# Folding the channels a second time ahead of a token transform, with the whole issue order from one table

## The chip, the core and the metric

The kernel runs on one core of a Trainium2 chip. A core has a matrix engine (TensorE, PE in the profile, with its weight loads as PEld), a vector engine (VectorE, DVE), a scalar engine (ScalarE, ACT), a general engine (GpSimd, POOL) and a queue engine that starts DMAs (SyncE, SP). Each works through its own list of instructions in order; semaphores tie them together. The metric is the device time of one launch in microseconds. The three runs of the kernel before have a median of 995.22 us (994.12 to 995.35).

## What is computed

Inputs are q, k, v of shape (8 batches, 8 heads, 576 tokens, 64), a gain g of 64 values and two weight matrices w1 (512 x 2048) and w2 (2048 x 512). The reference does, per batch:

```python
kv  = einsum('bhsd,bhse->bhde', k, v)
out = einsum('bhsd,bhde->bhse', q, kv)
x   = out / sqrt(mean(out*out, -1) + 1e-6) * g      # heads side by side: 576 x 512
X   = fft(fft(x, axis=tokens), axis=channels)
u   = x + real(X)
un  = (u - mean(u)) / sqrt(var(u) + 1e-6)
y   = u + maximum(un @ w1, 0) @ w2
```

The two transforms are done as matrix products with cosine and sine tables. Products that need more than one rounded 32-bit float (`fp32r` in the rows) are split into a high and a low part and done in three passes: high x high, high x low, low x high.

## The kernel before, in words

Eight batches go through an attention-and-transform stage of which PE does only a part, and 36 row tiles of 128 tokens go through the feed-forward stage (FFN), which is nearly all PE. Tokens are handled in nine blocks of 512. A block's "early" FFN work (three of the sixteen slices of the hidden layer) is issued between the steps of later batches; the other slices follow when all batches are done (from about 325 us on).

The steps of a batch, with the names that the rows use: `plan_kv` (L1197, `ps_k`) makes k-transposed times v; `plan_q` (L1273, L1279, `ps_q`) turns q; `plan_out` (L1304, `ps_o`; for the first batch `plan_first_out`, L1374) makes the attention output in three tiles t = 0, 1, 2 of 96 or 97 token pairs, a token s and its mirror 576 - s side by side in one row of the tile `x`; `plan_y` and L1490 normalise it. `plan_fold` then uses the symmetry of cosine and sine: L1501 (`ab`) adds channel d and channel 512 - d of the mirrored token, which leaves 256 channels; L1508 (`xe`, or `part` and `ps_xe`) makes the sum and the difference of the two tokens; L1514 and L1517 split them into high and low parts. A table called MODES says for each batch and tile whether L1508 and L1517 run on DVE (seven tiles) or on POOL (the other 17). L1495 on ACT keeps channel 0 apart for the mean (`x0`). `plan_seq` (L1532, for the first batch L1544) is the token transform: 290 columns, `ps_f<-cs`. Its result is split again into `pt`. `plan_chn` (L1586, `ps_f<-cd`) is the channel transform: for the cosine and for the sine part six matmuls with 128 rows, 96 or 97 weight columns and 258 moving columns. L1601 copies the cosine part, L1609 mixes cosine and sine parts with a sign into two results, L1619 and L1622 on POOL or L1628 and L1629 on DVE add them to `x`, and `plan_turn` (L1684, `ps_t`) turns the sum so that it becomes the input `unTh`, `unTl` (L1693, L1696) of the FFN, whose matmuls are L1012 (`ps_h`) and L1029 (`acc`), and in the late stage L2251.

`plan_spare` issues fill matmuls (L1084, `ps_s`), which compute nothing that is used. PE takes one when the planner has no better work ready.

The order is made when the program is built: every step is an `Op` with an engine, a cost and a rank; `Plan.go` plays the steps through in model time and takes for each free engine the ready step of lowest rank; MOVES shifts ranks, and SHIFTS moves single steps of the finished list or drops them.

## Time and profile before

| | |
|---|---|
| median of three runs | 995.22 us |
| profiled execution, span from first to last instruction | 993.5 us |
| PE busy in the span | 982.3 us, 99% |
| DVE, ACT, POOL busy | 690.1, 363.4, 397.6 us |
| fill matmuls (L1084) | 54 |
| channel transform matmuls (L1586) | 288, of 258 columns |

The span of the profiled execution is 1.7 us below the median of the runs, which also hold what lies before the first and after the last instruction. A matmul's busy time is its time from start to the modelled end, and matmuls overlap in the pipeline, so that the distance between starts, not the duration of one, tells how much of PE one matmul takes.

### The profile page before, as it was taken

What the parts mean: (1) busy time and instruction counts of PE and PEld (TensorE: products, weight loads), DVE (VectorE), ACT (ScalarE), POOL (GpSimd) and SP (SyncE); (2) the same over time, 40 slices, a digit from 0 to 9 for tenths busy, and PEclk for the clock granted to TensorE, in tenths of its full rate; (3) what the DMA queues carried; (4) which work ended last, traced back from release to release, by engine and by line L of the source; (5) the groups of instructions that cost most, each with busy time, mean ns of one, the idle gap of its engine ahead of it and who ended that gap; (6) DMA issues with size and microseconds to landing.
All of it is one profiled execution on the core that took longest, in us unless ns stands there. A gap on an engine that the chain in (4) does not pass through costs nothing.

```text
span 993.5 us, 17707 instructions
## 1 busy us (share of the span) xinstructions
PE 982.3 (99%) x6838; PEld 858.5 (86%) x6838; DVE 690.1 (69%) x1365; ACT 363.4 (37%) x731; POOL 397.6 (40%) x391
## 2 busy tenths in 40 slices
PE   8999999999999999999999999999999999999998
PEld 6888989988988888888888898989898888989897
DVE  4889886966667668767843786767676766767543
ACT  2466555655544333333332331323231313122221
POOL 1345443553554101434230372727272727263540
PEclk9899999999999999999999999999999999999999
DMA  9989797764453645565644515151525253424031
GB/s 231 236 222 271 210 275 230 200 161 165 144 195 117 267 168 192 181 252 211 225 170 159 201 44 212 44 212 53 202 81 187 100 171 115 153 107 149 1 127 43
DMA packets 111240, 166.06 MB, mean 167 GB/s; under 512 B 43710, under 2 KB 71666, under 8 KB 104756
## 3 DMA queue, kind: packets, MB, share of 16 engines
q1 hardware_dynamic: 103908, 149.06, 46.9%
q10 hardware_dynamic: 5328, 9.57, 2.6%
q0 software_dynamic: 1920, 6.29, 1.6%
q8 instruction: 54, 0.88, 0.4%
q14 instruction: 30, 0.25, 0.1%
HBM read 108.25 MB, written 56.64 MB: 166 GB/s over the span
## 4 chain that ended last, share of the span: by engine, by line
PE 94%; DMA 3%; SPq 1%; DVE 1%; issue 0%; ACT 0%; DVEq 0%; ACTq 0%
PE acc L1029 40%; PE ps_h L1012 20%; PE ps_h L2251 18%; PE ps_f L1586 4%; PE ps_f L1532 3%; PE ps_o L1304 3%; PE ps_k L1197 2%; PE ps_t L1684 2%; DMA vm<-in_v_dram 1%; PE ps_q L1279 1%; DMA draw<-in_dft_s_dram 1%; DMA qt<-in_q_dram 1%; PE ps_s L1084 1%; PE ps_o L1374 0%; SPq L1174 0%
## 5 line engine op out<-in xcount | busy, mean ns | idle before, releaser
L1029 PE MATMUL acc<-w,hh 128*128 128x512 f32 x1150 | 359.3, 394 | 0.0
L1029 PEld LDWEIGHTS acc<-w,hh 128*128 128x128 f32 x1150 | 205.7, 189 | 34.2
L1029 PE MATMUL acc<-w,hl 128*128 128x512 f32 x575 | 224.0, 390 | 0.0
L1021 ACT ACTIVATE hh<-ps_h 128x512 fp32r<-128x512 f32 x144 | 86.2, 598 | 345.8 <-DVE ps_h L2259 170.9
L1012 PE MATMUL ps_h<-unTh,w 128*128 128x512 f32 x576 | 179.3, 392 | 0.0
L1024 DVE SCALAR_TENSOR_TENSOR hl<-ps_h,hh 128x512 fp32r<-128x512 f32 x144 | 98.0, 684 | 92.1 <-ACT hh L1021 91.8
L1029 PEld LDWEIGHTS acc<-w,hl 128*128 128x128 f32 x575 | 108.0, 188 | 23.6
L1012 PEld LDWEIGHTS ps_h<-unTh,w 128*128 128x128 f32 x576 | 106.6, 188 | 21.3
L1012 PE MATMUL ps_h<-unTl,w 128*128 128x512 f32 x288 | 112.3, 390 | 0.0
L2211 POOL TENSOR_TENSOR up<-up 128x512 f32<-128x512 f32 x36 | 46.6, 1295 | 154.4 <-DMA up<-next_scr 119.2
L2259 DVE TENSOR_TENSOR ps_h<-part,ps_h 128x256 f32<-128x256 f32 x144 | 61.1, 425 | 40.9 <-ACT part L2264 23.3
L2259 DVE TENSOR_TENSOR part<-part,ps_h 128x256 f32<-128x256 f32 x108 | 45.4, 420 | 44.4 <-PE ps_h L2251 41.5
L1012 PEld LDWEIGHTS ps_h<-unTl,w 128*128 128x128 f32 x288 | 54.1, 188 | 11.5
L2224 POOL TENSOR_TENSOR uu<-uu,up 128x512 f32<-128x512 f32 x36 | 46.9, 1312 | 36.9 <-ACT up L2216 36.9
L1353 POOL TENSOR_TENSOR x<-x,gb 96x512 f32<-96x512 f32 (+1 forms) x26 | 33.8, 1311 | 45.0 <-ACT x L1320 45.0
L2264 ACT COPY part<-ps_h 128x256 f32<-128x256 f32 x36 | 13.4, 373 | 81.4 <-PE ps_h L2251 81.4
L1696 DVE TENSOR_TENSOR unTl<-ps_t,unTh 128x384 fp32r<-128x384 f32 (+13 forms) x80 | 34.0, 477 | 9.0 <-ACT unTh L1693 8.9
L2358 DVE SCALAR_TENSOR_TENSOR uu<-acc,bz,uu 128x512 f32<-128x512 f32 x35 | 25.0, 750 | 20.2 <-PE acc L1029 20.2
L1508 POOL TENSOR_TENSOR xe<-ab 96x256 f32<-96x256 f32 (+1 forms) x32 | 25.0, 797 | 34.0 <-DVE ab L1501 32.7
L1340 DVE TENSOR_REDUCE ss<-ps_o 96x8 f32<-96x512 f32 (+1 forms) x42 | 27.9, 682 | 14.1 <-ACT ps_o L1336 13.9
L1586 PE MATMUL ps_f<-cd,pt 128*96 128x258 f32 (+1 forms) x288 | 37.0, 283 | 0.0
L1586 PEld LDWEIGHTS ps_f<-cd,pt 128*96 128x96 f32 (+1 forms) x288 | 35.0, 162 | 1.3 <-DVE ss L1340 0.2
(226 smaller groups left out, 1875.9 us busy)
## 6 DMA issues: line engine op xcount, KB each, us to landing
raw<-in_moe_w_ch_dram SPq DMA_DIRECT2D x32, 512.0 KB, 3.9
unTh<-unT_scr SPq DMA_DIRECT2D x16, 1024.0 KB, 4.9
unTl<-unT_scr SPq DMA_DIRECT2D x16, 1024.0 KB, 7.3
qt<-in_q_dram SPq DMA_DIRECT2D x16, 576.0 KB, 6.7
unT_scr<-unTh SPq DMA_DIRECT2D x9, 1024.0 KB, 3.8
unT_scr<-unTl SPq DMA_DIRECT2D x9, 1024.0 KB, 7.3
part_scr<-part ACTq DMA_DIRECT2D x36, 256.0 KB, 4.0
next_scr<-part SPq DMA_DIRECT2D x36, 256.0 KB, 2.8
```

The source lines that it names most:

```text
L1012: nc.tensor.matmul(ps, w[c][:, kc * P : (kc + 1) * P], unT[a][:, kc, :], start=(kc == 0 and n == 0), stop=(kc == KC - 1 and n == 2),)
L1021: nc.scalar.activation(hh, ps, AF.Relu)
L1024: nc.vector.scalar_tensor_tensor(hl, ps, 0.0, hh.bitcast(F32), ALU.max, ALU.subtract)
L1029: nc.tensor.matmul(acc, hpair[a][:, i * P : (i + 1) * P], w[c], start=(first and n == 0), stop=(last and n == 2),)
L1304: nc.tensor.matmul(pss[s].t[:n, at : at + D], fqs[side].t[half, m, :n], kvt.t[half, m], start=True, stop=True,)
L1353: nc.gpsimd.tensor_tensor(v_, v_, gb[:n].unsqueeze(1).to_broadcast([n, H, D]), ALU.mult)
L1586: nc.tensor.matmul(ps.t[:n, :ND], pt.t[a][:, part, ch, offs[t] : offs[t] + n], cd[:, part, c, ch, :], start=(idx == 0), stop=(idx == 5),)
L1696: nc.vector.tensor_tensor(unTs[j].t[1][:, :, to], view()[:, :, lo:hi], unTs[j].t[0][:, :, to].bitcast(F32), ALU.subtract,)
L2211: lambda p=part: nc.gpsimd.tensor_tensor(p.t[:, 0], p.t[:, 0], p.t[:, 1], ALU.add),
L2224: lambda k=k, ut=ut, p=part: nc.gpsimd.tensor_tensor(ut.t[:, k], ut.t[:, k], p.t[:, 0], ALU.add),
L2251: nc.tensor.matmul(x(to), w.t[:, c, i, kk * P : (kk + 1) * P], rhs(a, kk), start=(kk == 0 and n == 0), stop=(kk == 1 and n == 2),)
L2259: return op("DVE", 415, URGENT, lambda: nc.vector.tensor_tensor(out(), a(), b(), ALU.add), d, bufs)
```

## The change

The channels are folded once more on the way into the token transform. After the first fold a tile has 256 channels; the change adds (and subtracts) channel m and channel 256 - m, which gives 128 channels for the even outputs and 128 for the odd ones. The token transform is as it was (two groups of 128 channels for each part). The channel transform has, for each part, three matmuls of 130 columns for the even outputs and three of 130 for the odd ones, in place of six of 258; each group of three now uses only one group of channels. Even and odd outputs lie apart in the PSUM bank and are brought together where L1601 and L1609 of before read them. The cosine and sine tables on the chip keep one group of 260 columns, rearranged to even and odd, with a correction of their last row on DVE. The value for the mean is now a sum of four channels on DVE in place of two on ACT. On the seven DVE tiles the last fold result lies in PSUM as before, and on the others in the buffer `ab`.

The planner with its ranks, shifts and model time is gone. The order of all steps is one list of numbers, read from first to last; steps that are not in it are not issued.

```diff
-SHIFTS = [
-    ("plan_spare.go/PE/-/-", 20, 0),
...
-MOVES = {
...
+ORDER = """
+5 242 222 389 215 234 226 213 4 38 18 13 26 23 25 390 391 392 0 227 216 2 209 219 211 218 212 401 210 208 221
...
     def run(self):
-        first = [o for o in self.ops if o.first]
...
+        seen = set()
+        line = [self.ops[int(n)] for n in ORDER.split()]
+        for o in line:
+            seen.add(o.n)
+            if any(a.n not in seen for a in o.after):
+                raise RuntimeError(f"{o.key} stands ahead of what it needs")
+        self.emit(line)
...
-    ND = DH + 2
+    ND = DH + 4
+    NH = ND // 2
...
-    cd = cst.tile([P, 2, 2, 2, ND], F32R, name="cd")
+    cd = cst.tile([P, 2, 2, 1, ND], F32R, name="cd")
...
+            def fit():
+                if part == 0:
+                    odd, far = raw.t[:, 1 : DH + 2 : 2], raw.t[:, DH + 3 : 2 * DH + 4 : 2]
+                    nc.vector.scalar_tensor_tensor(odd, far, last_row[:, 1:2], odd, ALU.mult, ALU.add)
+                nc.vector.tensor_scalar(raw.t[:, :ND], raw.t[:, :ND], last_row[:, 0:1], None, ALU.mult)
+
+            ld = [op("DVE", 600, r, fit, ld, [raw])]
...
         if quick:
-            ab, xe = e2_buf("ab"), bank_buf("ps_xe")
+            ab, xe = e2_buf("ab"), e2_buf("xe")
...
         def zero():
-            nc.scalar.activation(
-                x0[:n, t, b : b + 1], xv(0)[:, 0:1], AF.Identity, bias=xv(1)[:, 0:1]
-            )
+            nc.vector.tensor_reduce(x0[:n, t, b : b + 1], x.t[:n, :: DH], AX.X, ALU.add)
...
+        to = bank_buf("ps_xe") if quick else ab
+
+        def again(s):
+            def go():
+                o, a = two_of(to), two_of(xe)
+                m = P - s
+                eng.tensor_tensor(
+                    o[:, :, s * P : s * P + m], a[:, :, :m], a[:, :, DH - 2 : DH - 2 - m : -1],
+                    ALU.subtract if s else ALU.add,
+                )
+                if s:
+                    eng.tensor_copy(o[:, :, DH - 1 : DH], a[:, :, DH - 1 : DH])
+            return go
...
             def mm(part=part, ps=ps):
-                idx = 0
-                for ch in range(2):
-                    for a, c in passes:
+                for odd in range(2):
+                    ks = slice(odd * NH, (odd + 1) * NH)
+                    for i, (a, c) in enumerate(passes):
                         nc.tensor.matmul(
-                            ps.t[:n, :ND],
-                            pt.t[a][:, part, ch, offs[t] : offs[t] + n],
-                            cd[:, part, c, ch, :],
-                            start=(idx == 0),
-                            stop=(idx == 5),
+                            ps.t[:n, ks],
+                            pt.t[a][:, part, odd ^ part, offs[t] : offs[t] + n],
+                            cd[:, part, c, 0, ks],
+                            start=(i == 0),
+                            stop=(i == 2),
                         )
...
+        def bank_of(part):
+            return pss[part].t[:n, :ND].rearrange("p (r m) -> p m r", r=2)[:, : (W + 1) // 2]
...
-                    pss[s].t[:n, :W] if quick else pmv()[:, s], pss[1].t[:n, :W], sgn_t[:n, s, 0:1], me.t[:n, :W], ALU.mult, ALU.add
+                    to, bank_of(1), sgn_t[:n, s, 0:1], pairs_of(me), ALU.mult, ALU.add
```

The issue order changes on every engine. On PE, in the first batch, ahead of the first parts of the attention output (`ps_o`), these rows stood before (`ps_s` is the fill, `ps_k` the product of k and v, `ps_q` the turned q):

```order
L1197 MATMUL ps_k<-vr,kr 64x64 x2
L1084 MATMUL ps_s<-still 128x512 x6
L1197 MATMUL ps_k<-vm,km 64x64 x8
L1197 MATMUL ps_k<-vr,kr 64x64 x2
L1084 MATMUL ps_s<-still 128x512 x4
L1197 MATMUL ps_k<-vh,kh 64x64 x8
L1197 MATMUL ps_k<-vr,kr 64x64 x2
L1084 MATMUL ps_s<-still 128x512 x4
L1374 MATMUL ps_o<-kvt,fq 96x64 x16
L1374 MATMUL ps_o<-kvg,fq 96x64 x16
```

and these stand there now (lines of the changed kernel):

```order
L723 MATMUL ps_k<-vr,kr 64x64 x2
L723 MATMUL ps_k<-vh,kh 64x64 x8
L723 MATMUL ps_k<-vr,kr 64x64 x2
L900 MATMUL ps_o<-kvt,fq 96x64 x24
L900 MATMUL ps_o<-kvt,pt_190 96x64 x8
L799 MATMUL ps_q<-ident,qt 64x97 x8
L591 MATMUL ps_s<-still 128x512 x4
L900 MATMUL ps_o<-kvg,fq 96x64 x16
```

The fill between the useful matmuls is gone but for these four; 14 more stand at the very start, so that 18 are left of 54. The rest of PE's work ahead of the first FFN matmul (`ps_h`) is the same set of matmuls in another sequence, except for the 36 of the channel transform.

Those 36 begin, on PE in the first batch, like this before (`cd` is the table, `pt` the split result of the token transform):

```order
L1197 MATMUL ps_k<-vr,kr 64x64 x2
L1304 MATMUL ps_o<-kvt,fq 96x64 x16
L1304 MATMUL ps_o<-kvt,fq 97x64 x16
L1586 MATMUL ps_f<-cd,pt_688 96x258 x2
L1586 MATMUL ps_f<-cd,pt_689 96x258
```

and like this now:

```order
L723 MATMUL ps_k<-vr,kr 64x64 x2
L1127 MATMUL ps_f<-cd,pt_694 97x130 x2
L1127 MATMUL ps_f<-cd,pt_695 97x130
L1127 MATMUL ps_f<-cd,pt_694 97x130 x2
L1127 MATMUL ps_f<-cd,pt_695 97x130
```

The same number of matmuls, 130 columns wide, in the same pattern of two weights with the high and one with the low part. Every later batch has the same change.

On DVE, at the end of the first batch, where the low parts of the turned block (`unTl`) are made, these rows stood before:

```order
L1696 TENSOR_TENSOR unTl<-ps_t,unTh 128x4x74
L1446 RECIPROCAL rs_y<-rs_s 97x48
L1696 TENSOR_TENSOR unTl<-ps_t,unTh 128x4x21
L1696 TENSOR_TENSOR unTl<-ps_t,unTh 128x4x75
L979 TENSOR_TENSOR wa<-wa,ps_w 128x512
L1455 TENSOR_TENSOR ps_y<-rs_y,rs_s 97x48
L1490 TENSOR_TENSOR x<-x,ps_y 97x512 x2
L1490 TENSOR_TENSOR x<-x,ps_y 96x512
```

and these stand there now:

```order
L1016 TENSOR_TENSOR x<-x,ps_y 96x512
L1016 TENSOR_TENSOR x<-x,ps_y 97x512
L866 TENSOR_REDUCE ss<-ps_o 96x2x4 x2
L1247 TENSOR_TENSOR unTl<-ps_t,unTh 128x4x74
L1016 TENSOR_TENSOR x<-x,ps_y 97x512
L1247 TENSOR_TENSOR unTl<-ps_t,unTh 128x4x96
L1247 TENSOR_TENSOR unTl<-ps_t,unTh 128x4x21 x2
L1247 TENSOR_TENSOR unTl<-ps_t,unTh 128x4x75
L1247 TENSOR_TENSOR unTl<-ps_t,unTh 128x4
L1247 TENSOR_TENSOR unTl<-ps_t,unTh 128x4x96 x2
L1247 TENSOR_TENSOR unTl<-ps_t,unTh 128x4x74
L1247 TENSOR_TENSOR unTl<-ps_t,unTh 128x4x22
```

Three scalings of the second batch's tiles (`x<-x,ps_y`) stood behind the last low part and stand ahead of it now; so do the centring of a weight slice (`wa<-wa,ps_w`) and the product `ps_y<-rs_y,rs_s`, which now stand eight and five rows ahead of the first row shown.

## Rows read from the trace of the kernel before

**Rows 1.** The page: busy us, share of the span and instructions of PE.
```profile
PE 982.3 (99%) x6838; PEld 858.5 (86%) x6838; DVE 690.1 (69%) x1365; ACT 363.4 (37%) x731; POOL 397.6 (40%) x391
```

**Rows 2.** The page, chain that ended last: shares of the span by engine.
```profile
PE 94%; DMA 3%; SPq 1%; DVE 1%; issue 0%; ACT 0%; DVEq 0%; ACTq 0%
```

**Rows 3.** Busy time by stretch: PE, PEld, DVE, ACT, POOL (instructions), granted clock, DMA.
```profile
34.50:41.50 7.00, 7.00 (x72) 6.04 (x70) 5.21 (x12) 3.45 (x9) 2.83 (x3) 0.52 1.17 206
41.50:78.80 37.30, 36.80 (x566) 33.00 (x562) 33.54 (x67) 21.31 (x50) 16.78 (x22) 1.00 0.86 225
78.80:150.00 71.20, 71.20 (x751) 63.60 (x750) 62.06 (x130) 42.04 (x98) 35.36 (x50) 1.00 0.89 255
150.00:225.00 75.00, 75.00 (x750) 67.38 (x749) 53.42 (x105) 42.49 (x100) 34.97 (x41) 1.00 0.66 192
225.00:316.00 91.00, 91.00 (x632) 79.33 (x631) 62.35 (x128) 46.54 (x105) 41.91 (x48) 1.00 0.43 154
```

**Rows 4.** PE in order of time: start, us, instruction, idle before it and releaser.
```profile
33.35 0.81 PE L1374 MATMUL ps_o<-kvg,fq 64*97 64x64 f32 x13 [1.17 <-ACT fq L1283]
37.51 2.07 PE L1084 MATMUL ps_s<-still 128*128 128x512 f32 x4
...
78.81 0.73 PE L1012 MATMUL ps_h<-unTh,w 128*128 128x512 f32 x2
...
79.61 1.09 PE L1084 MATMUL ps_s<-still 128*128 128x512 f32 x4
```

**Rows 5.** The fill line L1084: count, duration ns, first and last start.
```profile
L1084 PE MATMUL ps_s<-still x54: 389/400/793, 1.7 to 255.3; 128*128 128x512 f32 x54
```

**Rows 6.** PE in order of time, a channel transform of one batch and what follows.
```profile
268.95 4.46 PE L1586 MATMUL ps_f<-cd,pt 128*97 128x258 f32 x36
273.25 0.62 PE L1029 MATMUL acc<-w,hh 128*128 128x512 f32 x2
```

**Rows 7.** PE in order of time, matmuls of 512 columns, three to a group.
```profile
81.22 0.62 PE L1012 MATMUL ps_h<-unTh,w 128*128 128x512 f32 x2
81.67 0.39 PE L1012 MATMUL ps_h<-unTl,w 128*128 128x512 f32 x1
81.90 0.62 PE L1012 MATMUL ps_h<-unTh,w 128*128 128x512 f32 x2
```

**Rows 8.** Weight loads by shape: count, busy us, mean ns of one.
```profile
L1012 PEld LDWEIGHTS ps_h<-unTh,w 128*128 128x128 f32 x576 | 106.6, 188 | 21.3
...
L1586 PEld LDWEIGHTS ps_f<-cd,pt 128*96 128x96 f32 x192 | 23.6, 162 | 0.8 <-DVE ss L1340 0.2
...
L1964 PEld LDWEIGHTS ps_o<-cs,x0h 96*8 96x8 f32 x4 | 0.4, 89 | 0.2
```

**Rows 9.** PE in order of time: 96 weight columns, 64 moving columns, two halves.
```profile
52.30 1.57 PE L1304 MATMUL ps_o<-kvt,fq 64*96 64x64 f32 x32
53.81 0.88 PE L1273 MATMUL ps_q<-ident,qt 96*64 96x96 f32 x16
```

**Rows 10.** PE in order of time: plain float32, 128 columns, 4 products in 8 records.
```profile
76.22 1.16 PE L970 MATMUL ps_w<-wa,mean_t 128*128 128x128 f32 x8
77.31 0.90 PE L1304 MATMUL ps_o<-kvt,fq 64*96 64x64 f32 x16
```

**Rows 11.** DVE in order of time, the last low part of the first batch.
```profile
78.36 0.68 DVE L1696 TENSOR_TENSOR unTl<-ps_t,unTh 128x84 fp32r<-128x84 f32 x2
```

**Rows 12.** DVE by line and shape: count, busy us, mean ns of one, idle before.
```profile
L1490 DVE TENSOR_TENSOR x<-x,ps_y 96x512 f32<-96x512 f32 x28 | 18.3, 675 | 0.0
...
L1455 DVE TENSOR_TENSOR ps_y<-rs_y,rs_s 97x48 f32<-97x48 f32 x7 | 1.6, 226 | 4.3 <-POOL fq L1289 3.5 <-POOL rs_s L1452 0.8
...
L1696 DVE TENSOR_TENSOR unTl<-ps_t,unTh 128x4 fp32r<-128x4 f32 x8 | 1.2, 156 | 0.0
```

**Rows 13.** The line L1508 on POOL and DVE: count, duration ns minimum, median, maximum.
```profile
L1508 POOL TENSOR_TENSOR xe<-ab x32: 720/734/1358, 33.4 to 298.9; 96x256 f32<-96x256 f32 x20, 97x256 f32<-97x256 f32 x12
L1508 DVE TENSOR_TENSOR ps_xe<-ab x14: 415/430/1395, 93.8 to 210.6; 96x256 f32<-96x256 f32 x12, 97x256 f32<-97x256 f32 x2
```

More of the change, by code (lines that the diff above doesn't have):

```diff
@@ L566 @@
+ORDER = """
[183 rows of a table added]
+"""
 class Buf:
@@ L604, in __init__ @@
         self.ops = []
-        self.now = 0
         self.where = ("-", "-")
@@ L609, in op @@
         o = Op()
-        o.port = port or eng == "POOL"
-        o.wait = wait
         o.eng, o.cost, o.emit, o.lag = eng, cost, emit, lag
@@ L615, in op @@
         o.key = (f"{what}/{b}", f"{what}/{b}/{t}")
-        o.rank = rank + sum(MOVES.get(k, 0) for k in o.key)
         o.after = [a for a in after if a is not None]
@@ L1109, in plan_dft, with taken, laid @@
                 ))
+        want = size
+        if key == "d":
+            want = ND
+            def fit():
[4 more added lines that the diff above has]
+            ld = [op("DVE", 600, r, fit, ld, [raw])]
+        def taken():
+            v_ = raw.t[:n, :want]
+            return v_.rearrange("p (m r) -> p r m", r=2) if key == "d" else v_
+        def laid(a):
+            return a.rearrange("p (r m) -> p r m", r=2) if key == "d" else a
         aside = MODES.get(f"high/{key}{part}", 0)
@@ L1626, in add_q @@
         def add_q(s):
-            v_, w = xv()[:, s], pss[1 - s].t[:n]
-            nc.vector.tensor_tensor(v_[:, :W], v_[:, :W], pss[s].t[:n, :W], ALU.add)
+            v_, w = xv()[:, s], mixed[1 - s].t[:n]
+            nc.vector.tensor_tensor(v_[:, :W], v_[:, :W], mixed[s].t[:n, :W], ALU.add)
             nc.vector.tensor_tensor(v_[:, W:], v_[:, W:], w[:, DH - 1 : 0 : -1], ALU.add)
         if quick:
-            adds = [op("DVE", 720, r, lambda s=s: add_q(s), pms, [x] + pss) for s in range(2)]
+            adds = [op("DVE", 720, r, lambda s=s: add_q(s), pms, [x, me] + pss, port=True) for s in range(2)]
         else:
```

712 lines of the change are left out of this document (25 added, 687 removed), and 182 rows, old and new, of the table ORDER.

## The prediction

> **What bounds the kernel now.** I read the page first. PE is busy for 982.3 of 993.5 us, and its share of the chain that ended last is 94% [rows 1, 2]: matmul time taken out counts nearly in full wherever PE is dense. The windows tell where that is. From 78.8 to 316 us PE's busy time equals the length of each stretch, at granted clock 1.00, with DVE at 62 of 71, 53 of 75 and 62 of 91 us and POOL at half or less [rows 3]. Ahead of 78.8 us the busy PE misleads. [...] The first FFN matmul starts at 78.81 us; of the 54 fill matmuls 48 stand ahead of it and 6 behind, four at 79.61 us and the last at 255.3 [rows 4, 5]. So I split the span: time = T1, the start of the first FFN matmul, plus PE's work behind T1. The first part is set by the chain, the second by how many matmuls there are and how far apart they start.
>
> **Channel transform.** 36 matmuls of 258 columns take from 268.95 to 273.25 us: 4.30 us, 119.4 ns each [rows 6]. At 512 columns three start in 0.68 us, 226.7 ns each [rows 7]. So a column costs (226.7 - 119.4)/254 = 0.422 ns, and 130 columns would stream in 119.4 - 128 x 0.422 = 65.3 ns. That is one end, if nothing else limits. But each matmul loads its own 96 or 97 weight columns. A load of 96 took 162 ns, one of 8 took 89 [rows 8], so a column adds 0.83 ns and 96 of them about 80 ns, more than the stream. The nearest row with as little streaming is the attention output: 96 weight columns, two halves side by side, 32 records in 1.51 us, thus 94 ns a pair, with the change of form at its end [rows 9]. I take 84 ns, close to the load's 80 and below the 94. The other end is far: a plain float32 product of 128 columns stands as two records, and seven of eight records take 1.16 - 0.288 = 0.87 us, 125 ns each or 250 ns a product [rows 10] (0.288 us is the mean duration of one). No fp32r matmul narrower than 256 columns is in the trace, so rows do not exclude that the narrow ones fall to this.
>
> Of 288 matmuls, 36 belong to the first batch, ahead of T1, where 36 x 35.4 ns = 1.3 us go into waits. The other 252 lie where PE is dense: 252 x (84 - 119.4) = **-8.9 us**. The ends are -13.6 us at 65.3 ns and +32.9 us at 250 ns; 94 ns would give -6.4.
>
> The row shows loads hidden under the running matmul: 119.4 ns is what 258 columns need, though 80 ns of load go with each [rows 6, 8]. [...]
>
> **Fill.** The six behind T1 go: 6 x 0.227 = **-1.4 us** [rows 5, 7]. The 30 that go ahead of T1 free gaps, not the chain.
>
> **T1.** The first batch's end is on DVE: its last low part starts at 78.36 us and the first FFN matmul follows at 78.81 [rows 4, 11]. DVE is busy for 33.54 of the 37.3 us from 41.5 to 78.8 [rows 3], so work put ahead of that low part moves T1. There are now three scalings of 0.675 us, one product of 0.226 and the centring, in whose place I set 0.68, a like 512-column operation: 2.9 us, which stood behind [rows 11, 12]. Added are three small reductions for the mean, about 0.156 each, and the correction of the table's last row, about two operations of 0.68: 1.8 us. Removed is half of the table's low part, some 0.7 us, and the table's high part on ACT shrinks likewise. That is +4.1 us on an engine with 3.8 us of idle time there. Also, the second fold of the first batch goes to POOL: per tile 2 x 0.734 us and a small copy, about 1.6 us [rows 12, 13], in series before `xh` can be made, with the token transform on PE queued behind it and the two other tiles behind it on POOL. Against that, the whole stretch is ordered anew, 30 fill matmuls no longer stand ahead of ready work, and the channel transform is 1.3 us shorter. From above +5 us if nothing is hidden; from below -4, about the idle time that DVE has there. I take **+1.0 us**, since most of it has idle time to go into.
>
> **Hidden behind T1.** DVE gets 14 second folds at 0.43 to 1.395 us (6.0 to 19.5), 7 small copies and 21 reductions at 0.156 (4.4), and the 42 mixes that read with a stride cost at most what a mirrored read costs more per element in these rows, 0.430/256 against 0.675/512 us, 0.09 each (up to 3.8): 10 to 28 us in all [rows 12, 13]. From 78.8 to 316 us DVE is idle for 9.1, 21.6 and 28.7 us [rows 3]; PE's queue of ready FFN slices hides this, so nothing. POOL gets 28 folds of 0.734, 20.6 us, and their small copies, against 125 us of idle time: nothing, except by the chains they lengthen, which FFN work covers. The table's loads shrink; ACT loses 24 small steps.
>
> **Sum.** 993.5 - 8.9 - 1.4 + 1.0 = 984.2 us of span. The median lies 1.7 us above the profiled span: 985.9, so I say **986.0 us**. Within this likeliest case 84 may be 94 or 70 ns and T1 move by some us: 980 to 992.
>
> **Rivals.**
> A: the weight load hides entirely, matmuls start every 65 ns, and the new order brings T1 forward by 2 us. For it: loads are hidden today [rows 6, 8]. Against: 80 ns of load do not fit under 55 ns of streaming. 993.5 - 13.6 - 1.4 - 2 + 1.7 = 978. [...]
>
> B: DVE paces the batches behind T1. Eight of the 14 second folds come in the stretch from 78.8 to 150 us; if each takes the longest 1.395 us of its line, with a third of the other 8.2 us, DVE needs 62.06 + 11.2 + 2.5 = 75.8 of 71.2 us [rows 3, 13]. PE is late by 4.6: 990.5. Against: the median is 0.430, not 1.395.
>
> C, the slower side: a narrow fp32r matmul is run like plain float32, 250 ns for 130 columns. 993.5 + 32.9 - 1.4 + 1.0 + 1.7 = 1027.7. The point where the change stops paying is 121 ns per matmul, only 1.6 ns above today's. For it: both kinds of product on few columns that the trace has, [rows 9, 10], are slower per column than the wide ones and no row has a single-pass product this narrow. Against: nothing in the rows says that the width, not the plain float32, makes the two records.
>
> D: load and stream add up, 135 ns: 993.5 + 3.9 - 1.4 + 1.0 + 1.7 = 998.7, slower too. Against: 119.4 ns today.
>
> E: with fill gone between the first matmuls PE is quieter, and the granted clock stays near the 0.52 seen at 34.5 to 41.5 us for another such stretch [rows 3]. If PE sets the pace in it, 7 us more: 993, no change. Against: PE mostly waits for others there.
>
> That the new order does less than the old cannot be: the matmuls other than fill are the same ones, but for their width.
>
> **Chances.** Forecast 0.50 (986), A 0.20 (978), B 0.08 (990.5), C 0.12 (1028), D 0.04 (998.7), E 0.06 (993). About 0.2%, 2 us, is what a measurement of this kernel tells from no change. Faster: 0.49 of the forecast, A whole, 0.06 of B, 0.02 of E, 0.77. Within 0.2%: 0.01, 0.02 of B, 0.03 of E, 0.06. Slower: C, D and 0.01 of E, 0.17. The range goes from 975, three below A, to 999, which takes in D; C is left out.
>
> **What would show it.** The distance between starts of the 130-column matmuls decides: near 84 the forecast, 65 A, 135 D, 250 C. The first FFN matmul should start at 79 to 81 us; later by 3 or more, with DVE or POOL as releaser, and the T1 term was wrong; a longer stretch at half clock ahead of it is E. Behind it PE's busy time should still equal each stretch's length and DVE rise to 75 to 90% before 150 us; idle PE with a DVE releaser there is B. If the span shrinks with spacing and T1 as said, the sum is right; if it shrinks elsewhere, it is wrong.

## The result and the profile after

The changed kernel takes 1005.55 us, the median of 16 runs (997.53 to 1011.0). The kernel before, in the same sessions, takes 995.41 us (993.93 to 997.27, 16 runs). The ratio is 1.009, its 95% interval 1.0068 to 1.0112: about 10 us slower, where 986.0 had been forecast. The profiled execution took 1004.67 us and its span is 1002.9.

The first two lines of the page of the changed kernel that matter, busy time by engine and the chain that ended last, answer to [rows 1, 2]:

```profile
PE 973.8 (97%) x6802; PEld 849.2 (85%) x6802; DVE 704.0 (70%) x1415; ACT 353.1 (35%) x707; POOL 419.3 (42%) x442
...
PE 86%; DVE 5%; DMA 4%; POOL 2%; issue 1%; ACT 1%; SPq 0%; DVEq 0%; POOLq 0%; ACTq 0%
```

PE has less to do, 973.8 us for 982.3. But it is idle for 1002.9 - 973.8 = 29.1 us where it was idle for 11.2. That is 17.9 us more idle time against 8.5 us less work, and the difference is the 9.4 us by which the span grew. DVE, DMA and POOL, together 4% of the chain before, hold 11% of it.

Where the idle time lies is read from the windows of the changed kernel: the stretches of [rows 3], then four short ones picked for their clock. The columns are as there (PE, PEld, DVE, ACT, POOL, granted clock, DMA share, GB/s).

```profile
34.50:41.50 7.00, 6.09 (x118) 5.60 (x114) 6.79 (x19) 2.32 (x7) 5.26 (x10) 1.00 0.92 273
41.50:78.80 37.30, 31.37 (x495) 28.36 (x495) 36.71 (x73) 22.63 (x50) 20.76 (x31) 0.95 0.77 193
78.80:150.00 71.20, 67.96 (x733) 60.48 (x733) 60.01 (x125) 36.27 (x81) 37.61 (x56) 0.91 0.86 234
150.00:225.00 75.00, 74.84 (x750) 65.41 (x749) 60.44 (x134) 42.11 (x95) 33.69 (x46) 1.00 0.77 211
225.00:316.00 91.00, 91.00 (x669) 79.20 (x668) 63.16 (x138) 44.23 (x101) 60.22 (x78) 1.00 0.42 147
10.00:16.50 6.50, 6.02 (x58) 5.83 (x60) 1.02 (x2) 0.00 (x0) 0.00 (x0) 0.50 1.07 235
75.00:85.00 10.00, 9.63 (x89) 8.54 (x90) 9.38 (x20) 3.00 (x7) 0.72 (x1) 0.50 0.33 102
127.00:132.50 5.50, 5.44 (x68) 5.13 (x70) 5.43 (x11) 3.03 (x8) 1.74 (x3) 0.50 0.79 249
464.00:467.00 3.00, 3.00 (x9) 2.33 (x8) 1.86 (x3) 1.07 (x2) 0.37 (x1) 0.50 0.96 311
```

From 41.5 to 78.8 us DVE is busy for 36.71 of 37.3 us, where it had 3.8 us of slack: by these numbers it is now the engine with least room there. From 78.8 to 150 us PE no longer fills its stretch. In four places the granted clock is 0.50; the kernel before has one such place, at 0.52, the first row of [rows 3].

PE in order of time, in the changed kernel, from the transform of the first batch to the first FFN matmul (`ps_h`), with the idle time before a group and its releaser in brackets:

```profile
73.58 0.55 PE L1235 MATMUL ps_t<-ident,x 96*128 96x96 f32 x4 [2.13 <-DVE x L1180]
75.37 0.91 PE L1235 MATMUL ps_t<-ident,x 97*128 97x97 f32 x4 [1.25 <-DVE ss L866]
...
79.38 2.87 PE L830 MATMUL ps_o<-kvt,fq 64*97 64x64 f32 x32
...
82.79 1.20 PE L516 MATMUL ps_h<-unTh,w 128*128 128x512 f32 x2
...
86.06 1.57 PE L830 MATMUL ps_o<-kvt,fq 64*96 64x64 f32 x32
```

The first FFN matmul starts at 82.79 us, 4.0 us later than in [rows 4]. It stands behind two waits for DVE, and the clock, 0.96 from 72 to 75 us, was 0.50 from 75 on: the 32 records at 79.38 take 2.87 us, a like 32 at 86.06, at full clock, 1.57.

The waits of PE in the whole of the changed kernel, longest first (us in total, times, longest):

```profile
PE ps_w L474 <- DVE wa L1294: 3.0, 1, 3.0
PE ps_t L1235 <- DVE unTl L1247: 2.9, 1, 2.9
PE acc L533 <- ACT part L1897: 2.4, 1, 2.4
PE ps_t L1235 <- DVE x L1180: 2.1, 1, 2.1
PE ps_k L723 <- DMA km<-in_k_dram: 1.9, 2, 1.4
PE ps_s L591 <- DVE still L583: 1.8, 1, 1.8
PE ps_h L516 <- ACT part L1420: 1.6, 1, 1.6
```

Three of them lie behind the first FFN matmul, in the stretch that the forecast took for full: the second ends at 127.06 us, the last at 363.18, the third at 462.81.

```profile
127.06 1.52 PE L1235 MATMUL ps_t<-ident,x 96*128 96x96 f32 x8 [2.94 <-DVE unTl L1247]
...
462.81 0.73 PE L533 MATMUL acc<-w,hh 128*128 128x512 f32 x2 [2.38 <-ACT part L1897]
```

At these two lie the last two of the stretches at clock 0.50; the first stretch lies at the longest wait of all, 3.0 us for `wa`. In the kernel before, the longest wait behind that point was 1.1 us:

```profile
PE ps_h L2251 <- DVE bz L2113: 1.1, 1, 1.1
```

The narrow matmuls themselves do what was forecast. PE in order of time, one run of 18 of them at full clock, and what follows:

```profile
238.41 1.67 PE L1127 MATMUL ps_f<-cd,pt 128*96 128x130 f32 x18
239.91 0.68 PE L533 MATMUL acc<-w,hh 128*128 128x512 f32 x2
```

(239.91 - 238.41)/18 = 83 ns each, against 119.4 in [rows 6] and 84 in the forecast. Load and stream one after the other, 80 + 55 = 135 ns by the forecast's estimates (55 for 130 columns at 0.422 ns), are not what the trace shows.

The last thing that the totals of the page hide is one form on DVE. The adds that end the transform (L1179, L1180) take one mixed output from PSUM (`ps_f`) and the other from the buffer `me` in SBUF. Count, duration in ns (minimum/median/maximum), first and last start, first of L1179, then of L1180:

```profile
L1179 DVE TENSOR_TENSOR x<-x,ps_f x8: 407/412/417, 67.2 to 209.1; 96x257 f32<-96x257 f32 x6, 97x257 f32<-97x257 f32 x2
L1179 DVE TENSOR_TENSOR x<-x,me x8: 412/420/1511, 69.3 to 212.2; 96x257 f32<-96x257 f32 x6, 97x257 f32<-97x257 f32 x2
```

```profile
L1180 DVE TENSOR_TENSOR x<-x,me x8: 409/418/1391, 67.6 to 209.4; 96x255 f32<-96x255 f32 x6, 97x255 f32<-97x255 f32 x2
L1180 DVE TENSOR_TENSOR x<-x,ps_f x8: 404/406/413, 69.6 to 212.6; 96x255 f32<-96x255 f32 x6, 97x255 f32<-97x255 f32 x2
```

The same add takes 0.40 to 0.42 us with an input in PSUM, always, and up to 1.51 us with both in SBUF. Of those 16, eleven take 0.41 to 0.44 us and five take 0.74 to 1.51, 4.2 us more in all. DVE in order of time, and then POOL in the same microseconds, show when:

```profile
70.40 1.39 DVE L1180 TENSOR_TENSOR x<-x,me 96x255 f32<-96x255 f32 x1
71.72 1.48 DVE L1179 TENSOR_TENSOR x<-x,me 97x257 f32<-97x257 f32 x1
73.12 0.40 DVE L1180 TENSOR_TENSOR x<-x,ps_f 97x255 f32<-97x255 f32 x1
```

```profile
70.10 1.41 POOL L1319 TENSOR_TENSOR w<-wa,w 128x512 fp32r<-128x512 f32 x1 [1.62 <-ACT w L1314]
...
71.52 2.82 POOL L879 TENSOR_TENSOR x<-x,gb 96x512 f32<-96x512 f32 x2
```

POOL's first operation ends at 71.51 us and the first of its next two at 71.52 + 1.41 = 72.93. DVE's two adds end at 71.79 and 73.20, each 0.27 to 0.28 us behind. So it is with all five: each starts while a two-input operation of POOL runs and ends 0.27 to 0.28 us behind its end. They waited for POOL's operation, and PE's wait of 2.13 us for `x` ends with the add behind them, at 73.52. The trace shows this on DVE's side, by the five adds; that POOL waits for DVE in turn is not shown here. In the kernel before, both mixed outputs lay in PSUM.

### The profile page after: what moved, and what is told of

Read it like the earlier page. It is cut to its first block, busy times and chain, and to the rows that moved or that the text cites. A ratio compares the mean times of both kernels' runs of the same rounds, so it can differ in the third digit from the quotient of the medians.

```text
span 1002.9 us, 17683 instructions
## 1 busy us (share of the span) xinstructions
PE 973.8 (97%) x6802; PEld 849.2 (85%) x6802; DVE 704.0 (70%) x1415; ACT 353.1 (35%) x707; POOL 419.3 (42%) x442
## 4 chain that ended last, share of the span: by engine, by line
PE 86%; DVE 5%; DMA 4%; POOL 2%; issue 1%; ACT 1%; SPq 0%; DVEq 0%; POOLq 0%; ACTq 0%
PE acc L533 38%; PE ps_h L1802 18%; PE ps_h L516 17%; PE ps_f L1073 3%; PE ps_o L830 3%; PE ps_f L1127 2%; PE ps_k L723 2%; PE ps_t L1235 2%; DMA qt<-in_q_dram 1%; DMA km<-in_k_dram 1%; PE ps_q L805 1%; DMA uu<-u_scr,rowidx 1%; DMA part_scr<-part 1%; DVE x L1180 1%; PE ps_o L900 0%
## 5 line engine op out<-in xcount | busy, mean ns | idle before, releaser
L1247 DVE TENSOR_TENSOR unTl<-ps_t,unTh 128x384 fp32r<-128x384 f32 (+14 forms) x80 | 34.2, 468 | 10.7 <-ACT unTh L1244 10.7
L450 DVE TENSOR_SCALAR ps_a<-ps_a 128x512 f32<-128x512 f32 x32 | 22.1, 693 | 26.4 <-ACT ps_a L443 26.4
L1244 ACT ACTIVATE unTh<-ps_t 128x384 fp32r<-128x384 f32 (+16 forms) x80 | 34.4, 496 | 15.6 <-PE ps_t L1235 14.4
L1319 POOL TENSOR_TENSOR w<-wap,w 128x512 fp32r<-128x512 f32 x10 | 12.9, 1292 | 62.0 <-ACT w L1314 62.0
```

Source lines behind the costliest of these rows:

```text
L1244: nc.scalar.activation(unTs[j].t[0][:, :, to], view()[:, :, lo:hi], AF.Copy)
L1247: nc.vector.tensor_tensor(unTs[j].t[1][:, :, to], view()[:, :, lo:hi], unTs[j].t[0][:, :, to].bitcast(F32), ALU.subtract,)
```

## The experiments

Times are medians; the ratio is to the kernel before in the same session (995.3 to 996.1 us), with its 95% interval, and is not the quotient of the two medians. Profiles are one execution each.

**The new fold in the old order** (e1). The arithmetic of the change, with its steps issued in the order of the kernel before and its 54 fills:

```diff
-ORDER = """   (the changed kernel's sequence)
+ORDER = """   (the sequence of the kernel before; each second fold behind its first fold)
```

> The second fold alone, with the issue order (and the fill) of the kernel before; its new steps stand right behind the first fold's. Theory O (the new order is what costs: less fill, waits of PE, then half clock; the fold by itself pays): the first FFN matmul at 79 to 82 us, no new waits of 2 us behind it, 252 matmuls 34 ns closer, so 985 to 991 us, 0.990 to 0.996 of the kernel before. Rival F (the fold's added work on DVE and POOL makes PE late in any order): 1000 us or more, with waits of PE on DVE and POOL between 78 and 160 us as in the changed kernel.

1017.79 us (1013.34 to 1023.44, 4 runs), ratio 1.0216 (1.016 to 1.0271). Its longest waits of PE:

```profile
PE ps_q L812 <- DVE x L1187: 3.3, 2, 2.1
PE ps_f L1080 <- DVE unTl L1254: 3.0, 1, 3.0
PE ps_q L812 <- DVE pm L1167: 2.9, 1, 2.9
```

With this fold the new order is not the worse one: in the old order the fold is 12 us slower still. PE waits for DVE, as the rival had it.

**The old fold in the new order** (e2): the steps of the kernel before, with its 258 columns, in the changed kernel's sequence, the second folds dropped from it.

```diff
-    ND = DH + 4
+    ND = DH + 2
...
-            ab, xe = e2_buf("ab"), e2_buf("xe")
+            ab, xe = e2_buf("ab"), bank_buf("ps_xe")
```

> The new order alone, with the channels folded once and matmuls of 258 columns as before. Theory O: waits and half clock as in the changed kernel and wide matmuls too, 1006 to 1014 us. Rival F: without the added work on DVE and POOL the order is no worse than the old one, 992 to 998 us.

1019.43 us (4 runs), ratio 1.0238 (1.0196 to 1.028). With e1 that makes a square: old fold in old order 995.4, new fold in old order 1017.8, old fold in new order 1019.4, both new 1005.6. Either part alone costs over 20 us. The sum of the two, 995.4 + 22.4 + 24.0 = 1041.8, isn't reached by 36 us: each sequence fits its own fold. The result lies above both expected ranges. It also lies some 13 us above what the runs below would give for it, 1005.9 without second folds (e5), 6.7 more for wide matmuls (e6) and 6.2 less with the mixes in PSUM (e7); no run explains that part.

**Fill back ahead of the first FFN matmul** (e3): 12 fill matmuls more, which ran from 77.37 us on.

```diff
@@ the table, PE, behind the transposes of the first batch @@
+ps_s <- still x8
...
+ps_s <- still x4
```

> The changed kernel with 12 fill matmuls put back where PE waits for the first batch's last sums: 8 ahead of the transposition that waited 2.13 us, 4 ahead of the one that waited 1.25 us. Theory C (part of the loss is the clock, which fell to half behind these two waits, from 75 to 85 us): granted clock 1.00 there, the first FFN matmul at 78 to 80 us in place of 82.8, total 4 to 6 us below the changed kernel, about 1000. Rival D (DVE's chain sets that point): clock or not, the first FFN matmul at 82 to 83 us and the total unchanged, 1004 to 1007.

1004.02 us (1003.34 to 1004.65, 4 runs), ratio 1.0082 (1.0055 to 1.0109). The waits for DVE stayed, now put down to the fill that stands in front (`ps_s <- DVE x` 2.1 us), and the first FFN matmul came at 87.78 us. The gain to the changed kernel, 1.5 us, lies inside the intervals. The fill did not hold the clock, which was 0.74 from 75 to 88 us (the eight fill matmuls from 77.37 us on start 0.50 us apart, for 0.227 in [rows 7]), so e3 doesn't show what full clock there would be worth; it shows that putting the fill back brings little.

**The kernel before without most of its fill** (e4):

```diff
+        fill = [o for o in line if o.key[0].startswith("plan_spare.go/PE")][9:]
+        line = [o for o in line if o not in fill]
```

> The kernel before with 18 fill matmuls at the start and the other 36 left out, in the old order and with the old fold. Theory C: the clock falls to half behind the waits of the first 80 us, the first FFN matmul comes 2 to 5 us later, 997 to 1001 us. Rival: fill does nothing but take 1.4 us of PE behind that point, 993 to 995 us.

996.93 us (10 runs), ratio 1.0013 (1.0 to 1.0026). Its windows ahead of 41.5 us:

```profile
0.00:34.50 34.50, 28.06 (x344) 25.04 (x346) 17.69 (x35) 12.23 (x23) 3.37 (x13) 0.79 0.98 246
34.50:41.50 7.00, 7.00 (x90) 6.88 (x90) 3.72 (x11) 3.10 (x8) 3.90 (x4) 0.50 0.98 210
```

The clock falls early without fill (0.79 in the first row, 1.00 before), and leaving the 36 fill matmuls out costs about 1.3 us in all (0 to 2.6), between the two expected ranges. The forecast had booked the six behind T1 as -1.4 us.

**The second folds left out** (e5), in the new order: the 48 operations at L1044 and their copies; the first fold writes where the second wrote.

```diff
         def again(s):
             def go():
-                o, a = two_of(to), two_of(xe)
...
+                return None
```

> The changed kernel in its own order without the 48 second folds (and their 24 small copies): the first fold's result goes into the transforms as it is, so that the output is not the reference's; matmuls are as narrow as in the changed kernel. Theory S (the second fold's own steps on DVE and POOL lengthen the chains until PE waits): the waits before 130 us shrink, 985 to 995 us. Rival (the new order waits at these places anyway): 1000 to 1006 us.

1005.9 us (1000.81 to 1011.56, 4 runs), ratio 1.0118 (1.0073 to 1.0163): no gain, though DVE and POOL have 6.5 and 23 us less to do. In the new order the second folds aren't what PE waits for, as far as four runs with 11 us between them can tell.

**The transform at 260 columns** (e6), in the new order:

```diff
-                    ks = slice(odd * NH, (odd + 1) * NH)
+                    ks = slice(0, ND)
```

> The changed kernel with its own order, but each matmul of the channel transform takes all 260 columns of the table in place of 130 (the output is not the reference's). If PE is dense where they stand, the whole forecast term comes back: 252 x 35 ns = 8.9 us, 1013 to 1016 us. If PE waits for others there, the narrow matmuls only made the waits longer and the wide ones cost little: 1005 to 1010 us.

1012.28 us (4 runs), ratio 1.0162 (1.0127 to 1.0197). In this order the narrow matmuls are worth 6.7 us, between the two expectations.

**Both mixed outputs in PSUM** (e7), in the new order:

```diff
-        mixed = [pss[0], me]
+        def mixed(s):
+            return pss[0].t[:n, s * 254 : s * 254 + W + 1]
```

> The changed kernel with both mixed results of the DVE tiles in PSUM, as in the kernel before, in place of one in PSUM and one in SBUF (four columns of one result are overwritten). Theory P (an add on DVE with both inputs in SBUF waits for POOL: 1.2 to 1.5 us in place of 0.40, five times in the first batch): these adds take 0.4 us, the first batch's sums come 3 us earlier, 1000 to 1003 us. Rival (those waits are hidden by others): 1004 to 1007 us.

999.36 us (995.26 to 1003.31, 10 runs), ratio 1.0033 (1.0012 to 1.0053). Groups of DVE by line in its trace: all 32 adds are short again.

```profile
L1181 DVE TENSOR_TENSOR x<-x,ps_f 96x257 f32<-96x257 f32 (+1 forms) x16 | 6.6, 413 | 0.1
L1182 DVE TENSOR_TENSOR x<-x,ps_f 96x255 f32<-96x255 f32 (+1 forms) x16 | 6.5, 409 | 0.0
```

16 adds that read both inputs from SBUF cost 6.2 us of the whole, more than the 4.2 us by which they are longer on DVE, and the forecast didn't have this term. (Of the five long adds three lie in the first batch, not five as the expectation has it.) The first FFN matmul starts at 79.40 us here, 3.4 earlier, but one execution doesn't settle that, as e12 shows.

**The old order without second folds** (e9): e1 with the edit of e5.

```diff
         def again(s):
             def go():
-                o, a = two_of(to), two_of(xe)
...
+                return None
```

> As the second fold in the old order, but without the 48 second folds and their small copies (the output is not the reference's); narrow matmuls, the sum for the mean on DVE and the mixes stay as in the change. Theory S: the 22 us that the fold cost in the old order go, and the narrow matmuls pay: 985 to 992 us. Rival (other parts of the change, such as the sums on DVE or adds that wait for POOL, hold the old order up): 1005 us or more.

998.03 us (996.44 to 1005.08, 10 runs), ratio 1.0032 (1.0012 to 1.0051). The result lies between the two expectations. In the old order the second folds cost 1017.8 - 998.0 = 19.8 us, in the new one nothing (1005.9 to 1005.6). But without them the new order is 7.9 us slower than the old.

**The old order, no second folds, both mixes in PSUM** (e11): e9 with the edit of e7. What is left of the change is the narrow matmul, the strided reading, the mean and the table.

```diff
-        mixed = [pss[0], me]
+        def mixed(s):
+            return pss[0].t[:n, s * 254 : s * 254 + W + 1]
```

> The old order without the second folds, and with both mixed results in PSUM (the output is not the reference's): of the change the narrow matmuls, the rearranged table and the sums for the mean on DVE are left. Theory N (the narrow matmuls are worth what was forecast where PE is dense, and the adds with both inputs in SBUF hid it): 8.9 us below the kernel before, 985 to 989 us. Rival (the narrow matmuls gain little, since others pace PE): 992 to 997 us.

993.4 us (990.1 to 995.0, 10 runs), ratio 0.9967 (0.9955 to 0.998). Faster than before, but by 2.6 us, as the rival had it. The adds are worth 4.6 here (998.0 to 993.4).

**The narrow matmuls alone** (e18): the kernel before, in its own order, with 130 and 128 columns; half of each sum is left out.

```diff
-                            ps.t[:n, :ND],
+                            ps.t[:n, ks],
...
-                            cd[:, part, c, ch, :],
+                            cd[:, part, c, ch, ks],
```

> The kernel before with narrow channel transforms and nothing else: each matmul writes 130 or 128 columns in place of 258, same count, same order, fill and folds (the output is not the reference's, as half of each sum is missing). Theory N (the forecast's first term, 252 x 35 ns where PE is dense): 8.9 us less, 985.5 to 988 us; the matmuls 83 to 86 ns apart. Rival (other engines pace the batches so closely that PE gains only waits): 990 to 995 us, with new waits of PE between 80 and 300 us.

991.15 us (989.06 to 992.75, 6 runs), ratio 0.9955 (0.9943 to 0.9967): -4.2 us, not -8.9, as the rival had it. They start 84 ns apart here too (36 from 268.12 to 271.16 us). The windows of this kernel, as in [rows 3], and one of its waits:

```profile
78.80:150.00 71.20, 70.01 (x778) 61.88 (x778) 62.60 (x134) 41.96 (x99) 36.32 (x51) 1.00 0.90 256
150.00:225.00 75.00, 74.10 (x757) 65.86 (x756) 54.20 (x107) 42.91 (x100) 34.98 (x41) 1.00 0.65 193
```

```profile
PE ps_q L1279 <- DVE x L1627: 1.5, 2, 1.0
```

Where PE had been busy for the whole of 71.2 and 75 us it is now idle for 1.2 and 0.9. From 78.8 to 316 us the 252 matmuls of the channel transform are busy for 23.3 us, before for 32.2, so the 8.9 us are there; but others were close behind PE. These 2.1 us of waits end on loads, ACT, POOL and DVE by turns, the longest, 0.57 us at 174.62, on DVE; the other wait for `x`, 0.97 us at 70.10, stands ahead of the first FFN matmul, which starts 1.5 us later here, at 80.30. Where the rest of the 4.7 us went is not traced.

**Mending three places of the new order** (e12). On DVE a low part (`unTl`) stands ahead of a fold and a scaling; on ACT each store of `part` follows its own copy; on SP some stores stand ahead of weight loads. In the order of DVE and of ACT:

```order
+L1248 TENSOR_TENSOR unTl<-ps_t,unTh 128x4x96
 L1026 TENSOR_TENSOR ab<-x 96x512
 L1022 TENSOR_REDUCE x_110<-x 96x1
 L1033 TENSOR_TENSOR xe<-ab 96x256 x2
 L851 TENSOR_TENSOR x<-ps_o,gb 97x4x64 x4
-L1248 TENSOR_TENSOR unTl<-ps_t,unTh 128x4x96
```

```order
-L1421 COPY part<-acc 128x512 x2
-L1425 DMA part_scr<-part 128x512 x2
+L1421 COPY part<-acc 128x512
+L1425 DMA part_scr<-part 128x512
+L1421 COPY part<-acc 128x512
+L1425 DMA part_scr<-part 128x512
```

> The changed kernel with the three mended places of the order alone, mixes as in the change. Theory: the wait of 2.9 us at 124 us, the half clock behind it (5.6 us at half, 2.8 us lost) and the waits of 2.0 us at 361 us go: 998 to 1000 us. Rival: the waits move on, 1003 to 1006 us.

999.63 us (997.59 to 1001.76, 5 runs), ratio 1.0043 (1.0029 to 1.0058): 5.9 us less than the changed kernel. Its longest waits:

```profile
PE ps_w L475 <- DVE wa L1295: 3.3, 1, 3.3
PE ps_t L1236 <- ACT fq L810: 2.3, 1, 2.3
PE ps_t L1236 <- DVE x L1181: 2.1, 1, 2.1
PE acc L534 <- ACT part L1898: 2.1, 1, 2.1
```

The wait for `unTl` has gone but for 0.8 us and one of 2.3 us for `fq` has come a little earlier, at 122.75; that for `part` of 1.6 us has gone; that for the later `part` is still there, mended or not. All the moved steps stand behind the first FFN matmul, so the waits there cost whole microseconds, which the forecast had set at nothing.

This run shows one thing more. Up to the first FFN matmul its list is that of the changed kernel, adds included, and still that matmul starts earlier, with the clock low for a shorter time:

```profile
75.00:85.00 10.00, 10.00 (x163) 8.81 (x163) 9.71 (x21) 3.01 (x8) 0.73 (x1) 0.87 0.72 169
```

```profile
79.80 0.70 PE L517 MATMUL ps_h<-unTh,w 128*128 128x512 f32 x2
```

So that point moves by 3 us and more from one execution of the same list to the next.

**Both mends together** (e10): the second mixed output in a PSUM bank of its own, the three places of e12, and two small moves that the bank needs.

```diff
-        mixed = [pss[0], me]
+        mixed = [pss[0], bank_buf("ps_m") if quick else None]
```

> The changed kernel with two edits and a full result: on the DVE tiles the second mixed result gets a PSUM bank of its own, so that no add there has both inputs in SBUF; and three places of the order are mended (on DVE one low part of the turned block ahead of a fold, at 122 us; on ACT two stores of partial sums right behind their copies, and on SP four stores ahead of two weight loads, both for the wait at 361 us). Theory (these waits and the half clock behind them are the loss): 1005.5 - 6.2 for the adds - 2.9 and about 2.5 of half clock at 124 us - 2.0 at 361 us = 992, 988 to 995 us, a little faster than the kernel before. Rival (a wait that is taken away comes back at the next place): 997 to 1001 us.

1002.14 us (998.41 to 1012.08, 10 runs), ratio 1.0072 (1.0044 to 1.01). 12 us were not to be had by adding e7 and e12, and the result lies above both expected ranges. (It is not quite their sum: the bank of its own and the two moves are new.) In the profiled execution the first FFN matmul starts at 75.82 us, 7 us earlier than in the changed kernel's, and all of it is given back: the wait below and the window behind it. In e13, with the same list up to there, it starts at 84.02.

```profile
PE ps_t L1236 <- ACT fq L810: 4.1, 1, 4.1
```

```profile
78.80:150.00 71.20, 65.45 (x661) 58.60 (x660) 55.32 (x115) 34.25 (x76) 37.19 (x55) 0.86 0.82 218
```

**More places mended**, with the bank (e13) and without (e14): for `fq`, two squares and a store go behind a copy of the turned q and a high part on ACT, and a scaling behind a low part on DVE; four late stores go ahead of loads on SP, as here in the order of SP.

```order
-L441 DMA raw<-in_moe_w_ch_dram 128x4x256
-L1901 DMA next_scr<-part 128x512
+L1901 DMA next_scr<-part 128x512 x2
+L441 DMA raw<-in_moe_w_ch_dram 128x4x256
```

> The second mixed result in a bank of its own and the three mended places as before, and two more: on ACT a copy of the turned q and a high part of the turned block ahead of two squares, and a store of partial sums behind them (the wait of 4.1 us at 119 us, in which ACT stood at that store); on SP, in four places, the store of the partial sum that is copied first ahead of the one copied second (the wait of 2.2 us at 461 us). Theory (the waits and the half clock behind them can be taken out): 1002.1 - 4.1 - about 3 of half clock - 2.2 - about 1.7 of half clock = 991, 988 to 995 us, faster than the kernel before. Rival (in this order each wait taken away returns elsewhere, since the first batches have no slack): 998 to 1002 us.

> The changed kernel with all five mended places of the order, mixes as in the change. Theory: 999.6 (three places) - 2.3 at 120 us - 2.1 and some half clock at 453 us = 994 to 996 us. Rival: 998 to 1001 us.

999.31 us (997.75 to 1006.71, 12 runs), ratio 1.0044 (1.0024 to 1.0064), and 1000.28 us (993.62 to 1005.92, 11 runs), ratio 1.0031 (1.0007 to 1.0055). No better than e12 or e7. In e14's profile the first centring product waited long, and the first FFN matmul came at 90.45 us, though its list up to there is still that of the changed kernel:

```profile
PE ps_w L475 <- DVE wa L1295: 6.2, 1, 6.2
```

Behind that point the same execution needed only 910.5 us, against 920.1 in the changed kernel. So a late start can be made up in part, as an early one can be lost.

**More fill early** (e15 alone, e17 with the places of e14, e16 with the bank too): 44 fill matmuls more than the changed kernel, 62 in all: 12 more at the start, 20 between there and 50 us, and the 12 of e3.

```diff
@@ the table, PE, first batch @@
-ps_s <- still x14
+ps_s <- still x26
...
+ps_s <- still x4
```

> The changed kernel with 44 fill matmuls put back where PE waits in the first 75 us (12 ahead of the first centring product, for which PE waited 3.0 us at 7 us, 20 in waits from 16 to 45 us, 12 in the two waits at 71 to 75 us); nothing else is moved. Theory C (in the new order PE's own work up to the first FFN matmul is near the path, so half clock there delays that point, by more or less from run to run): clock 1.00 from 10 to 78 us, the first FFN matmul at 78 to 81 us in every execution, 999 to 1002 us and runs within 6 us of each other, where the changed kernel's span 13.5. Rival (other engines set that point): 1003 to 1007 us and the same spread.

> The version with the second mixed result in a bank of its own and five mended places, with the same 44 fill matmuls. Its profile had the clock at 0.75, 0.50 and 0.87 in the three stretches up to 78.8 us, and the first FFN matmul at 84.0, with 75.8 us in a run of the same early order at 0.90, 1.00 and 1.00. Theory C: that point at 75 to 77 us in every execution, 990 to 995 us, faster than the kernel before. Rival: 997 to 1001 us.

> The changed kernel with five mended places and the same 44 fill matmuls, mixes as in the change. Theory C: the first FFN matmul at 78 to 81 us (90.5 in the profile without fill, at clock 0.74, 0.50 and 0.83), 994 to 997 us. Rival: 999 to 1002 us.

1003.85 (6 runs; 1.0107, 1.0083 to 1.0132), 1004.19 (6; 1.0085, 1.0069 to 1.0102) and 1002.98 us (6; 1.0073, 1.0056 to 1.0091). No gain to speak of: e15 lies 1.7 us below the changed kernel, but e16 lies 4.9 above e13 and e17 2.7 above e14, the same versions without this fill, and both above their expected ranges. The fill did raise the clock, to a mean of 0.985 to 0.997 in these 18 runs, where the changed kernel's 16 have 0.971 to 0.991. In e16 PE waited for loads instead:

```profile
PE ps_k L724 <- DMA vr<-in_v_dram: 2.8, 1, 2.8
```

**All mends, a little fill** (e19): e13 with 16 fill matmuls more and the first centring product behind the first turns of q, so that its wait delays nothing.

```order
+L800 MATMUL ps_q<-ident,qt 64x96 x40
 L475 MATMUL ps_w<-wa,mean_t 128x128 x4
-L800 MATMUL ps_q<-ident,qt 64x96 x40
```

> A version with a full result: second mixed result in a bank of its own, five mended places, the first centring product of PE behind the turns of the first q (PE waited 3 to 6 us for it at 7 us), and 16 fill matmuls in waits that end on DVE and ACT (at 29, 39, 45 and 75 us). If what is left is the start of the first batch and the clock from 30 to 60 us: the token transform begins at 46 to 48 us, the first FFN matmul at 75 to 77, 993 to 997 us. Rival (DVE and the loads pace the first three batches, so that an earlier start only comes back as waits behind it): 998 to 1002 us.

1001.37 us (998.06 to 1007.39, 6 runs), ratio 1.0083 (1.0061 to 1.0105). Its waits, longest first:

```profile
PE ps_q L800 <- DMA qt<-in_q_dram: 2.4, 2, 1.8
PE ps_k L724 <- DMA km<-in_k_dram: 2.0, 1, 2.0
```

The wait for `wa` has gone and loads have taken its place. No version that computes the whole result beat the kernel before; e13, e12 and e14, at 999.3 to 1000.3 us, come nearest.

## Why the prediction was wrong

**The distance of the narrow matmuls** was right: 83 ns for 84, a value picked between estimates of 80 and 94. With that the rivals that went by another distance are out: A (65 ns), D (135) and C (250). No run shows D's 135 ns or the +3.9 us that it stands for, 252 times the 15.6 ns above the 119.4 of before: the matmuls start 83 ns apart here and 84 in e18. The kernel is slower, but not by C or D, the ways in which the forecast had seen it slower.

Split at T1, the start of the first FFN matmul, as the forecast split it, the profiled execution has T1 at +4.0 us for +1.0, and behind it 1002.9 - 82.79 = 920.1 us for 993.5 - 78.81 = 914.7: +5.4 us where -8.9 - 1.4 had been booked. PE is idle there for 12.5 us, before for 5.0.

**The first step that failed: "The other 252 lie where PE is dense: -8.9 us."** e18 does this edit and nothing else, and gives -4.2 us. The matmuls shrank by the 8.9 us, but the dense stretches did not stay dense: PE waits for 2.1 us between 78.8 and 225 us where it had not waited, by turns for loads, ACT, POOL and DVE. That PE is busy for the whole of a stretch says that PE is the last, not by how much. The term should have had the slack of the next engine as a bound.

**The second: "PE's queue of ready FFN slices hides this, so nothing."** This was said of 10 to 28 us more on DVE. Two things were wrong with it.
One is the price. The adds were left at their old 0.41 us, while for half of them the change moves one of the two inputs from PSUM to SBUF; that stands in its code (`mixed = [pss[0], me]`), in a line that the part of the diff shown above leaves out. Beside a POOL operation such an add takes up to 1.51 us. [rows 13] had the warning, a DVE operation with two SBUF inputs at 1.395 us for a median of 0.430; in that trace six of its 14 take 0.77 to 1.395 us, each ending 0.29 us behind a POOL operation. e7 against the changed kernel (6.2 us) and e11 against e9 (4.6) show what that costs in either order.
The other is the cover. In the trace nothing queued behind a waiting transpose went ahead of it: while one waited 2.94 us for `unTl`, up to 127.06, PE started nothing, the next products for `ps_k` not before 128.51 and the next FFN slices not before 142.17. Waits of 2.9, 2.4 and 1.6 us came out of this, each longer than any behind the first FFN matmul before, and e12 takes 5.9 us back by moving a few instructions. The forecast named rival B for it, DVE as the pace of the batches, and B's sign is there, idle PE with DVE as releaser before 150 us (2.94 us at 127.06). But it priced B at 4.6 us by DVE's busy time (in that sum a third of 8.2 us stands as 2.5 and is 2.7). DVE's busy share before 150 us, 60.01 of 71.2 or 84%, is even inside the 75 to 90% that had been called harmless, and below the 62.06 us of [rows 3]. Shares don't show it; the place of one instruction in a queue does.

**T1.** The sum had +5 us "if nothing is hidden", and +1.0 was taken. In the profiled execution it was 82.79 - 78.81 = +4.0, by the forecast's own sign a miss: DVE is busy for 6.79 + 36.71 = 43.50 us from 34.5 to 78.8 where [rows 3] give 38.75. The direction was right, and the engine with 3.8 us of idle time in 37.3 had no room for 4. Of DVE's extra time 2.8 us are three of the held adds, which the forecast didn't have; and behind them PE ran at a clock of 0.50 from 75 to 85 us. How much each is worth isn't settled, for with the same list T1 was 79.80 in e12, just the +1.0 of the forecast, and 90.45 in e14. A hit there would have been luck.

**Fill.** The -1.4 us weren't there, since e4 loses 1.3 us without the fill. Rival E, the clock, is seen ahead of T1: 0.50 from 10 to 16.5 and from 75 to 85 us. But fill that raised the clock brought 1.7 us back in e15 and cost 4.9 and 2.7 in e16 and e17, so the missing fill is not the loss.

**The sum by the runs.** Along one path each step but the first is one edit: 995.4 before, 993.4 with the narrow matmuls, the strided reading, the mean and the table in the old order, without second folds (e11), 998.0 with the adds on SBUF (e9), 1005.9 in the new order (e5), 1005.6 with the second folds (after). Along the other the second folds add 19.8 us in the old order (e1) and the new order takes 12.2 of them back. So the new order makes room for the second folds, and it pays for that with waits of its own: 7.9 us (998.0 to 1005.9), more than the narrow matmuls give. The terms depend on each other: e7 and e12 gain 6.2 and 5.9 us alone, and together, in e10, 3.4.

**What stays open.** Why mends don't add up: an early start is lost again behind it (e10), a late one partly made up (e14), and on which of DVE, ACT, POOL and the loads the first batches then hang differs from run to run. Why the new order spreads so widely, 13.5 us over 16 runs against 3.3 before: the arrival of the early loads with DVE full is a guess that no run isolates. What the record does show is that time and clock go together: the six fastest of the 16 runs have a mean granted clock of 0.986 to 0.991, the six slowest 0.971 to 0.985. Which of the two leads is not shown; the waits stand at the stretches of low clock, and the fill of e15 to e17 raised the clock with little or no gain in time.

## What to carry to other kernels

An engine that is busy for all of a stretch is the last one, not the only one: before a cut on it is booked in full, ask who comes next and how much slack stands between, and where that isn't known, take the full sum for an upper bound; here less than half of it came (4.2 of 8.9 us). In a queue that runs in a fixed order, work added to a second engine is not hidden by ready work that stands behind the waiting instruction (here PE stood still for 2.94 us at one transpose); follow each added operation to the instruction that waits for it, and see what is queued there. When a change moves an operand from PSUM to SBUF, price the operations that read it anew, beside what POOL does in those microseconds (here an add of 0.41 us took up to 1.51); and when order and arithmetic change together, run both mixed versions, since neither part alone tells what the other is worth.

## What the runs showed of the hardware

- An add on DVE of 255 or 257 columns took 0.41 us with an input in PSUM (all 32 of e7). With both inputs in SBUF it took 0.41 to 0.44 us where at its start no two-input POOL operation ran or one had at most 0.15 us to go, and 0.74 to 1.51 where one had 0.46 to 1.23 us to go (five of 16), ending 0.27 to 0.28 us behind that one's end. Six of the 14 operations on DVE in [rows 13] did the same in the kernel before, at 0.29 us.
- Of 18 matmuls of 130 columns with 96 weight columns each, at full clock, one starts every 83 ns; a load takes about 80 ns and the stream 65 by the forecast's estimates from [rows 6, 7, 8], so by these the load and not the stream sets the distance; no run isolates it.
- In the changed kernel a wait of PE of 2.1 to 3.0 us stands at each of four stretches at half clock (about 7, 10, 7 and 3 us long); at the wait of 1.58 us that ends at 363.18 none is seen. The length of the wait alone doesn't tell: in the kernel before such a stretch of about 7 us follows a wait of 1.17 us at 33.35 ([rows 3, 4]). The 32 records of one attention part took 2.87 us in one and a like 32 took 1.57 outside.
